# Two layers behind a causal attention on one core: layer 2's first product reads its tokens and its weights from tiles declared early in SBUF

## The chip, the cores and the metric

The kernel runs on one core of a Trainium2 chip. Its time is the device time of one execution in microseconds (us). Of the kernel before there are three timed runs and one profiled execution.

## The reference

Three stages in float32, cut to what is computed:

```
x = causal attention(q, k, v) with decay f      # 4 batches x 8 heads x 576 x 64
x = x as [2304 tokens, 512]
h = x @ w_in                                     # layer 1: 512 -> 1024
solu = h * softmax(h);  ln = layernorm(solu) * g_ln
x = ln @ w_out                                   # 1024 -> 512
h = max(x @ moe2_w_in, 0)                        # layer 2: 512 -> 2048
out = (h * h) @ moe2_w_out                       # 2048 -> 512
```

## The kernel before

Every float32 product is made of three matmuls of rounded halves (high x low, low x high, high x high), so a tile of operands always comes as an h and an l. Layer 2 works on blocks of TB = 256 tokens with Strassen-like products of blocks, which is why its weights are prepared as seven sums per unit (w2u in DRAM, 128x512 each) and its down weights as sums in w2d, w2f and w2s.

**Order.** Nothing is issued as the program text stands. Each piece of work is added to a `Plan` with costs, a due time (`prio`), the keys that it reads and writes, and the ring slots that it takes. `pl.lay` then simulates the five engines and writes one order for each; DMAs all go through SyncE's queue (SP). A changed key, ring size or cost can therefore move instructions on all engines.

**Layer 2** is made of four kinds of work:
- `half_up(p)` (matmul at L1300), eight of them: the first block's up product. Moving operands are XOP[5] and XOP[6] (tiles vn0 to vn3); weights are pieces of `HU`: first six pieces of `upper`, then wil, k20, k21, pt, e.
- `unit(b, p)`, 32 of them: seven products of six 128x256 matmuls each (`mm`, L1347). The stationary operand is a piece of the ring `upper`, loaded from w2u by the DMA at L1336; the moving operand is XOP[i], the token operand i of the block of tokens. Products 0 and 1 are opened together (`open2`: one matmul of product 1, the six of product 0, the other five of product 1). VectorE adds results out of PSUM (L1373), ScalarE and GpSimd make relu and square; a result takes a slot of the ring RQ.
- `step(blk, p)`, 72 of them: VectorE forms sums of a result (L1418) and its halves (L1111, `k<-adj,k` for the S half, `ln<-q,ln` for the A half), then TensorE does seven down products of three 128x256 matmuls (L1448, L1449, L1450). Stationary: GA (in ln1) or GS (in k11). Moving: halves of the down weights, in pieces of wih, free, woh, wil, k20, k21, pt, e, ws, q3, qn, xc and one last small piece of k11.
- `x_block(b)`: loads and splits the token operands of a block of 512 tokens into XOP (L1191 and behind).

**Where things lie.** Layer 2 has no tiles of its own. `carve` cuts pieces out of tiles of the earlier stages, and `once`/`claim` make the first user of a piece wait until the earlier stage's keys on it (`held`) are done. All tiles come from one pool with one buffer each, and lie in SBUF in the order of their declaration; in bytes of a partition:

| tiles, in order | bytes | role in layer 2 |
|---|---|---|
| maskb; wih, wil, woh | 1152; 2496 to 51648 | W2 pieces (moving) |
| wol; k20, k21, qn | 51648 to 92608 | XOP[1] to XOP[4]; W2 pieces |
| vn0 to vn5, kn0, kn1 | 92608 to 108992 | XOP[5], XOP[6]; raw loads |
| pt, e | 108992 to 125888 | W2 pieces, half_up weights |
| q2 | 125888 to 134080 | four RQ slots |
| free, ws, xc, q3 | 134080 to 158144 | W2 pieces |
| adj, xh, xl, ident, xw, x, q1 | 158144 to 182144 | sums, seven RQ slots, raw loads |
| k10, k11 | 182144 to 204672 | `upper`, GS |
| ln0, ln1 | 204672 to 229248 | `upper`; GA, one `upper` piece, XOP[0] |

In names of the trace the digits at a tile's end are cut: `k` is any of k10, k11, k20, k21, and `ln` is ln0 or ln1. Before the change `upper` has 13 pieces: five of k10, GS[4] of k11, six of ln0, GA[4] of ln1. Product i of unit n uses piece (7n + i) mod 13. XOP[0] is GA[5:7], the last 4096 bytes of ln1.

```
K1 = [new(f"k1{j}", [HH, KW], F32R) for j in range(2)]
GA = carve("ln1", [384] * 4 + [512] * 3)
XOP[0] = GA[5:7]
m = (7 * n + i) % NU
```

Of the kernel before, what the change touches and what calls it, by code (L numbers as in the profile page):

```python
# [240 lines left out]
def tile_kernel(ctx: ExitStack, tc: tile.TileContext, q, k, v, f, w_in, w_out, g_ln, w2_in, w2_out, out):  # L241
# [76 lines left out]
    X = new("x", [NP, P])  # L318
    Q1 = [[new(f"q1{i}{j}", [HH, P], F32R) for j in range(2)] for i in range(2)]
    K1 = [new(f"k1{j}", [HH, KW], F32R) for j in range(2)]  # L320
    for y in range(2):
        new(f"ln{y}", [KF * 3 * P])
    LN = {}
    XC = {}
    Z = [ps.tile([P, 512], F32, name=f"z{i}") for i in range(2)]
# [1 line left out]
    HP = ps.tile([P, 2, 512], F32, name="hp")  # L327
    PP = [ps.tile([P, 512], F32, name=f"pp{i}") for i in range(3)]

    NU, NRQ = 13, 11  # L330
    pl = Plan(dict(pp=3, hp=2, rq=NRQ), ("z0", "z1", "xo", "h", "h0", "h1"))
    uid = [0]

# [393 lines left out]
    def weights1(prio_in, prio_out):  # L727
        ws = {}
        n = 0

        for c in range(2):
            for r in range(KC):
                i = n % 4
                w = slice(c * 512, (c + 1) * 512)

                def stage(i=i):
                    tag = f"ln{i // 2}"
                    if tag not in ws:
                        ws[tag] = new(tag, [KF * 3 * P])
                    return ws[tag][:, (i % 2) * 1536 : (i % 2) * 1536 + 1536]  # L740

                convert(
                    w_in[r * P : (r + 1) * P, w].bitcast(U32), lambda stage=stage: stage()[:, 0:1024],
                    lambda stage=stage: stage()[:, 1024:1536], lambda r=r, w=w: wih[:, r, w],
                    lambda r=r, w=w: wil[:, r, w], 512, prio_in + n * PIN, ("lnr", i), ("lnw", i), ("wi", r, c),
                )
                n += 1
        for g in range(2 * KF):
            j, c = divmod(g, 2)
            i = g % 2  # L750
            w = slice(c * 256, (c + 1) * 256)

            def stage(i=i):
                tag = ("xc", "ws")[i]
                if tag not in ws:
                    ws[tag] = new(tag, [768])
                return ws[tag]

            convert(
                w_out[j * P : (j + 1) * P, w].bitcast(U32), lambda stage=stage: stage()[:, 0:512],  # L760
                lambda stage=stage: stage()[:, 512:768], lambda j=j, w=w: woh[:, j, w],
                lambda j=j, w=w: wol[:, j, w], 256, prio_out + g * POUT, ("wsr", i), ("wsw", i), ("wo", j, c),
                gain=gcol[:, j : j + 1],
            )
        return ws


    def out1(blk, ccs, prio, dp):
# [3 lines left out]
        for cc in ccs:  # L772
            w = slice(cc * P, cc * P + P)
            sk = key()
            for g in range(4):
                def fn(g=g, sk=sk, w=w):
                    px = at(sk)[:, 0 : 2 * P].rearrange("p (r x) -> p r x", x=P)
                    for fc in (2 * g, 2 * g + 1):
                        hi = LN["h"][:, fc, ring[0] : ring[1] + 1 : step, :]
                        lo = LN["l"][:, fc, ring[0] : ring[1] + 1 : step, :]  # L780
                        nc.tensor.matmul(px, lhsT=woh[:, fc, w], rhs=lo, start=(fc == 0), stop=False)  # L781
                        nc.tensor.matmul(px, lhsT=wol[:, fc, w], rhs=hi, start=False, stop=False)  # L782
                        nc.tensor.matmul(px, lhsT=woh[:, fc, w], rhs=hi, start=False, stop=(fc == KF - 1))  # L783
# [31 lines left out]
    def first(x):  # L815
# [82 lines left out]
        for g in range(KF // 4):  # L898
            ck = key()

            def flips(g=g, ck=ck):
                if not LN:
                    LN["h"], LN["l"] = (new(f"ln{y}", [KF, 3, P], F32R) for y in range(2))
                tp = at(ck).rearrange("p (c x) -> p c x", x=P)
                for c in range(4):
                    cc = 4 * g + c
# [1 line left out]

            def lo(g=g, ck=ck):
                nc.vector.tensor_tensor(  # L910
                    out=LN["l"][:, 4 * g : 4 * g + 4, x % 3, :], in0=at(ck).rearrange("p (c x) -> p c x", x=P),
                    in1=LN["h"][:, 4 * g : 4 * g + 4, x % 3, :].bitcast(F32), op=ALU.subtract,
                )

# [29 lines left out]
    for nm, a in (("h", "woh"), ("l", "wol")):  # L944
        held[a] = [("wo", fc, y, nm) for fc in range(KF) for y in range(2)]
    held["ln0"] = [("lnh", y, z) for y in range(3) for z in range(2)]
    held["ln1"] = [("lnl", y, z) for y in range(3) for z in range(2)]
    held["e"], held["x"] = ["e"], ["x"]
    held["xh0"], held["xl0"] = [("xh", 0, o) for o in (0, 64)], [("xl", 0, o) for o in (0, 64)]
    held["ws"] = [("wsr", 1, z) for z in "lh"] + [("wsw", 1)]  # L950
# [42 lines left out]
    upper += carve("k10", [512] * 5)  # L993
    GS = carve("k11", [512] * 5 + [256])
    upper += GS[4:5] + carve("ln0", [512] * 6)
    GA = carve("ln1", [384] * 4 + [512] * 3)
    upper += GA[4:5]
    XOP[0] = GA[5:7]
    at_h = len(large)
    more("wil", 8)  # L1000
    for j in range(2):
# [5 lines left out]
    more("qn", 0, 2)  # L1007
    more("xc", 0, 3)
    small += GS[5:]
    RQ = [carve(a, [512], F32)[0] for a in ["xl0", "xh0", "adj2"] + [f"q1{i}{j}" for i in range(2) for j in range(2)]]  # L1010
    RQ += carve("q2", [512] * 4, F32)
    U2 = [carve(a, [256], F32)[0] for a in ("xw", "maskb")]
    KP = KF2 // 2
    HU = upper[:6] + large[at_h:]
# [266 lines left out]

    def new_r(sg, p, prio):
        for x, y in enumerate(RQ):
            once(("rq", x), y, ["rqs"], prio)
        uid[0] += 1
        rslot[sg, p] = ("rq", uid[0])
        return rslot[sg, p]
# [25 lines left out]
    def unit(b, p, prio):  # L1313
# [12 lines left out]
        def half(i):  # L1326
            o = uprods[i]
            return psum(ks[o[0]])[:, o[1] * TB : o[1] * TB + TB]

        def weights(i, prio):  # L1330
            m = (7 * n + i) % NU
            sk = ("us", m)
            if sk not in first_use:
                once(sk, again(upper[m]), [sk], prio)
            pl.add(
                dict(dma=LOAD2), lambda: nc.sync.dma_start(upper[m][0]().bitcast(F32), w2u[p, i]), prio - UAHEAD,  # L1336
                [("w2u", p, i)], [sk],
            )
            return [sk, ("xo", i, 0), ("xo", i, 1)]

        def mm(i, a=0, e=6, start=-1):
            u, xh, xl = upper[(7 * n + i) % NU][0](), XOP[i][0][0](), XOP[i][1][0]()
            for j in range(a, e):
                c, k = divmod(j, 3)
                wh, wl = u[:, c * P : c * P + P], u[:, 256 + c * P : 256 + c * P + P]
# [272 lines left out]
            first(tiles[n]["x"])  # L1618


    t0 = TEND + P2
    t1 = t0 + KP * 2800
    x_half(t0 - W2X)
# [110 lines left out]
```

## Time and profile before

| | |
|---|---|
| three runs | 836.78, 838.57, 839.84 us; median 838.57 |
| profiled execution | 837.13 us, span 835.3 us |
| mean granted TensorE clock | 0.994 of full speed |
| TensorE (PE) busy | 791.1 us, 95% of the span, 6392 matmuls |
| weight loads (PEld) busy | 720.6 us, 86% |
| VectorE (DVE) busy | 635.1 us, 76% |
| ScalarE (ACT) busy | 549.3 us, 66% |
| GpSimd (POOL) busy | 394.3 us, 47% |
| chain that ended last | PE 69%, ACT 11%, DVE 8%, DMA 4% |

Attention and layer 1 run interleaved up to 488 us, with the eight half_up products between 453 and 488; from there on only layer 2 is left. A matmul's duration in a row includes the pipeline, so consecutive matmuls overlap; the pace is read from the distance of their starts.

### The profile page before, as it was taken

How to read it: one execution, taken by the hardware profiler on the slowest of the kernel's cores; microseconds unless marked ns; L12 is line 12 of the kernel's file. 1: busy time of each engine (PE TensorE's matmuls, PEld its weight loads, DVE VectorE, ACT ScalarE, POOL GpSimd, SP SyncE). 2: the span in 40 equal slices, each digit the busy share in tenths (PEclk: the TensorE clock that was granted, in tenths of full speed). 3: DMA queues.
4: the chain of work that ended last, by engine and by line, in shares of the span. 5: the costliest groups of instructions: out<-in, count | busy, mean ns of one | idle time of the engine just before them, and what ended most of it. 6: DMA issues, size and time to landing. Idle time of an engine off the chain costs nothing.

```text
span 835.3 us, 18703 instructions
## 1 busy us (share of the span) xinstructions
PE 791.1 (95%) x6392; PEld 720.6 (86%) x6392; DVE 635.1 (76%) x1614; ACT 549.3 (66%) x1414; POOL 394.3 (47%) x544
## 2 busy tenths in 40 slices
PE   4877899999999999999999998999999999999997
PEld 2555688888888788888889998999999999999997
DVE  8798867977867567776757789778778877977776
ACT  6899988888888888998866665444334433533342
POOL 6468777666688766798677310020211121112110
PEclk9999999999999999999999999999999999999999
DMA  6644346556655454655557789976766757665401
GB/s 204 207 135 127 110 122 202 176 170 203 182 177 191 153 185 133 208 201 189 198 181 230 250 284 345 319 259 212 218 191 232 234 180 230 203 209 180 162 8 44
DMA packets 109663, 159.66 MB, mean 191 GB/s; under 512 B 12832, under 2 KB 52768, under 8 KB 109568
## 3 DMA queue, kind: packets, MB, share of 16 engines
q1 hardware_dynamic: 109568, 158.47, 59.3%
q8 instruction: 50, 0.82, 0.4%
q14 instruction: 45, 0.37, 0.2%
HBM read 121.65 MB, written 36.72 MB: 190 GB/s over the span
## 4 chain that ended last, share of the span: by engine, by line
PE 69%; ACT 11%; DVE 8%; DMA 4%; POOL 3%; issue 3%; SPq 0%; DVEq 0%; POOLq 0%; ACTq 0%
PE z L1347 9%; PE pp L1347 9%; PE pp L592 5%; PE xo L612 5%; PE z L538 4%; PE hp L1449 3%; PE hp L1448 3%; PE hp L1450 3%; PE hp L830 3%; PE hp L832 3%; PE hp L831 3%; ACT adj L573 2%; PE pp L781 2%; PE pp L783 2%; PE pp L782 2%
## 5 line engine op out<-in xcount | busy, mean ns | idle before, releaser
L573 ACT ACTIVATE adj<-z,st 64x288 f32<-64x288 f32 (+9 forms) x192 | 95.3, 500 | 13.1 <-DVE st L559 9.7
L538 PE MATMUL z<-k,q 80*64 80x288 f32 (+17 forms) x384 | 93.9, 345 | 9.0 <-DVE q L503 8.3
L592 PE MATMUL pp<-ident,adj 128*128 128x128 f32 (+1 forms) x480 | 82.0, 282 | 17.0 <-ACT adj L573 15.7
L592 PEld LDWEIGHTS pp<-ident,adj 128*128 128x128 f32 (+1 forms) x480 | 52.1, 144 | 44.4 <-ACT adj L573 27.7
L559 DVE CUSTOM_DVE_ANT_0 z<-z,maskb 128x128 f32<-128x128 f32 (+8 forms) x144 | 65.5, 464 | 29.5 <-PE z L538 27.6
L781 PE MATMUL pp<-ln,woh 128*128 128x256 f32 x288 | 83.9, 291 | 1.5 <-DVE ln L910 1.5
L347 ACT COPY pt<-pp 128x256 f32<-128x256 f32 (+5 forms) x170 | 69.0, 419 | 18.8 <-PE pp L592 17.6
L1111 DVE TENSOR_TENSOR k<-adj,k 128x512 fp32r<-128x512 f32 x75 | 52.6, 701 | 37.7 <-POOL k L351 28.2
L783 PE MATMUL pp<-ln,woh 128*128 128x256 f32 x288 | 80.7, 280 | 0.0
L782 PE MATMUL pp<-ln,wol 128*128 128x256 f32 x288 | 80.7, 280 | 0.0
L538 PEld LDWEIGHTS z<-k,q 128*128 128x128 f32 (+3 forms) x384 | 58.1, 188 | 15.9 <-ACT pt L1554 8.2
L351 POOL TENSOR_SCALAR ln<-q 128x384 fp32r<-128x384 f32 x31 | 16.9, 545 | 107.0 <-PE hp L1450 45.8
L705 POOL TENSOR_TENSOR free<-free 128x256 uint32<-128x256 uint32 x64 | 50.5, 796 | 35.4 <-DVE free L699 28.6
L830 PE MATMUL hp<-wih,xl 128*128 128x512 f32 x144 | 62.1, 431 | 2.8 <-ACT hp L869 2.8
L612 PE MATMUL xo<-pt,vn 128*64 128x128 f32 (+1 forms) x960 | 63.8, 274 | 0.5 <-ACT pt L347 0.3
L612 PEld LDWEIGHTS xo<-pt,vn 128*64 128x64 f32 x960 | 50.6, 140 | 11.5 <-issue 6.1
L351 POOL TENSOR_SCALAR k<-adj 128x512 fp32r<-128x512 f32 x38 | 23.7, 622 | 75.1 <-DVE adj L1418 30.3
L781 PEld LDWEIGHTS pp<-ln,woh 128*128 128x128 f32 x288 | 54.8, 190 | 4.4 <-DVE ln L910 1.8
L831 PE MATMUL hp<-wil,xh 128*128 128x512 f32 x144 | 56.9, 395 | 0.2 <-DVE wil L709 0.2
L832 PE MATMUL hp<-wih,xh 128*128 128x512 f32 x144 | 56.9, 395 | 0.0
L782 PEld LDWEIGHTS pp<-ln,wol 128*128 128x128 f32 x288 | 55.0, 191 | 0.4
L783 PEld LDWEIGHTS pp<-ln,woh 128*128 128x128 f32 x288 | 54.8, 190 | 0.0
(580 smaller groups left out, 2636.3 us busy)
## 6 DMA issues: line engine op xcount, KB each, us to landing
ln<-w2u SPq DMA_DIRECT2D x119, 256.0 KB
k<-w2u SPq DMA_DIRECT2D x105, 256.0 KB
w2u<-free SPq DMA_DIRECT2D x56, 256.0 KB
kn<-in_k_dram SPq DMA_DIRECT2D x32, 256.0 KB
free<-in_moe_w_out_dram SPq DMA_DIRECT2D x32, 256.0 KB
free<-in_moe_w_in_dram SPq DMA_DIRECT2D x32, 256.0 KB
w2f<-free SPq DMA_DIRECT2D x49, 128.0 KB
vn<-in_v_dram SPq DMA_DIRECT2D x20, 256.0 KB
```

Of the source, the lines that this page charges most:

```text
L347: nc.scalar.copy(dst(), src())
L538: nc.tensor.matmul(dst, lhsT=ql[0:r, p, 0:m], rhs=rhs, start=(g == 0), stop=(g == 1))
L573: nc.scalar.activation(out=adj[0:m, c[1] : c[2]], in_=Z[c[0]][0:m, 0 : c[2] - c[1]], func=AF.Exp, bias=st[0:m, low : low + 1], scale=-1.0, ...
L592: nc.tensor.transpose(at(sk)[:, (c - g) * m : (c - g + 1) * m], adj[0:m, zc : zc + P], ident[0:m, 0:m])
L612: nc.tensor.matmul(XO[own[j], g // 2, off : off + m], lhsT=VN[vslot[b, c]][:, (g + j) * D : (g + j + 1) * D], rhs=PT[(s - h + g + j) % NPT ...
L781: nc.tensor.matmul(px, lhsT=woh[:, fc, w], rhs=lo, start=(fc == 0), stop=False)
L782: nc.tensor.matmul(px, lhsT=wol[:, fc, w], rhs=hi, start=False, stop=False)
L783: nc.tensor.matmul(px, lhsT=woh[:, fc, w], rhs=hi, start=False, stop=(fc == KF - 1))
L830: nc.tensor.matmul(HP[:, c], lhsT=XL[i][:, cc, :], rhs=wih[:, cc, w], start=(cc == 0), stop=False)
L831: nc.tensor.matmul(HP[:, c], lhsT=XH[i][:, cc, :], rhs=wil[:, cc, w], start=False, stop=False)
L832: nc.tensor.matmul(HP[:, c], lhsT=XH[i][:, cc, :], rhs=wih[:, cc, w], start=False, stop=(cc == KC - 1))
L1347: nc.tensor.matmul(half(i), lhsT=l, rhs=r[:, c * TB : c * TB + TB], start=(j == start), stop=(j == 5), skip_group_check=True,)
```

## The change

Three homes are moved. XOP[0], the moving operand of product 0, goes from ln1 to the second half of q2. The weights of product 0 leave the ring: unit n loads them into one of two pieces in the first half of q2 (`lower[n % 2]`). The ring `upper` keeps products 1 to 6 with 12 pieces (the piece in ln1 is dropped); product i uses piece (6n + i - 1) mod 12. In exchange RQ loses its four slots in q2 and gets three in ln1, ten in all in place of eleven; these three come first in the list and are held by empty steps until layer 1 ends. For that, ln1 is split in two tiles, ln1a (GA) and ln1b (RQ), at the same addresses, and layer 1's low half LN["l"] is a list of the two.

```diff
-    for y in range(2):
-        new(f"ln{y}", [KF * 3 * P])
+    new("ln0", [KF * 3 * P])
+    for y in "ab":
+        new(f"ln1{y}", [KF // 2 * 3 * P])
...
-    NU, NRQ = 13, 11
+    NU, NRQ = 12, 10
...
-                        lo = LN["l"][:, fc, ring[0] : ring[1] + 1 : step, :]
+                        lo = LN["l"][fc // 4][:, fc % 4, ring[0] : ring[1] + 1 : step, :]
...
-    held["ln1"] = [("lnl", y, z) for y in range(3) for z in range(2)]
+    for z in range(2):
+        held["ln1" + "ab"[z]] = [("lnl", y, z) for y in range(3)]
...
     GS = carve("k11", [512] * 5 + [256])
     upper += GS[4:5] + carve("ln0", [512] * 6)
-    GA = carve("ln1", [384] * 4 + [512] * 3)
-    upper += GA[4:5]
-    XOP[0] = GA[5:7]
+    GA = carve("ln1a", [384] * 4)
+    c = carve("q2", [512] * 4)
+    lower, XOP[0] = c[:2], c[2:]
...
-    RQ = [carve(a, [512], F32)[0] for a in ["xl0", "xh0", "adj2"] + [f"q1{i}{j}" for i in range(2) for j in range(2)]]
-    RQ += carve("q2", [512] * 4, F32)
+    RQ = carve("ln1b", [512] * 3, F32)
+    LATE = len(RQ)
+    RQ += [carve(a, [512], F32)[0] for a in ["xl0", "xh0", "adj2"] + [f"q1{i}{j}" for i in range(2) for j in range(2)]]
...
         for x, y in enumerate(RQ):
-            once(("rq", x), y, ["rqs"], prio)
+            if x >= LATE:
+                once(("rq", x), y, ["rqs"], prio)
...
+        def place_of(i):
+            if i == 0:
+                return ("ul", n % 2), lower[n % 2]
+            m = (6 * n + i - 1) % NU
+            return ("us", m), upper[m]
+
         def weights(i, prio):
-            m = (7 * n + i) % NU
-            sk = ("us", m)
+            sk, piece = place_of(i)
             if sk not in first_use:
-                once(sk, again(upper[m]), [sk], prio)
+                once(sk, again(piece), [sk], prio)
             pl.add(
-                dict(dma=LOAD2), lambda: nc.sync.dma_start(upper[m][0]().bitcast(F32), w2u[p, i]), prio - UAHEAD,
+                dict(dma=LOAD2), lambda: nc.sync.dma_start(piece[0]().bitcast(F32), w2u[p, i]), prio - UAHEAD,
                 [("w2u", p, i)], [sk],
             )
...
-            u, xh, xl = upper[(7 * n + i) % NU][0](), XOP[i][0][0](), XOP[i][1][0]()
+            u, xh, xl = place_of(i)[1][0](), XOP[i][0][0](), XOP[i][1][0]()
...
+    late = [("rq", f"late{x}") for x in range(LATE)]
+    for k_ in late:
+        pl.add(dict(dve=0), lambda: None, -9.1e6, [], [], take=k_)
+    pl.add(dict(dve=0), lambda: None, TEND, [], list(RQ[0][1]), uses=late)
```

Line numbers shift with it: L1336 becomes L1347, L1347 becomes L1358, L1448 to L1450 become L1459 to L1461, L1111 becomes L1116, L1373 becomes L1384, L1418 becomes L1429.

**TensorE, the opening of the first unit.** First as it stands before (the name ahead of the arrow is the PSUM bank, behind it the moving and the stationary tile):

```order
2326 L1347 MATMUL z_120<-wol_5725,k_49_5115 128x256
2327 L1347 MATMUL z_120<-ln_49_5597,k_49_5115 128x256 x6
2328 L1347 MATMUL z_120<-wol_5725,k_49_5115 128x256 x5
2329 L1347 MATMUL z_121<-wol_5725,k_49_5115 128x256 x12
2330 L1347 MATMUL z_120<-wol_5725,k_49_5115 128x256 x6
2331 L1347 MATMUL pp_126<-wol_5725,ln_49_5773 128x256
2332 L1347 MATMUL pp_126<-ln_49_5597,ln_49_5773 128x256 x6
2333 L1347 MATMUL pp_126<-wol_5725,ln_49_5773 128x256 x5
```

And now:

```order
2326 L1358 MATMUL z_121<-wol_5731,k_50_5121 128x256
2327 L1358 MATMUL z_121<-q_50_5025 128x256 x6
2328 L1358 MATMUL z_121<-wol_5731,k_50_5121 128x256 x5
2329 L1358 MATMUL z_122<-wol_5731,k_50_5121 128x256 x12
2330 L1358 MATMUL z_121<-wol_5731,k_50_5121 128x256 x6
2331 L1358 MATMUL pp_127<-wol_5731,ln_50_5779 128x256
2332 L1358 MATMUL pp_127<-q_50_5025 128x256 x6
2333 L1358 MATMUL pp_127<-wol_5731,ln_50_5779 128x256 x5
```

The six matmuls of product 0 stand at the same place, between the first and the other five of product 1. Before they read ln (XOP[0]) against weights in k (unit 0) or ln (unit 1); now both operands are in q2, which the row names once. Over the program TensorE has the same matmuls; their order differs within the first four units only, and from there to the end it is the same.

**SyncE's queue, the loads of product 0's weights for units 0 and 1.** Before, around the first loads of layer 2's down weights:

```order
302 L1131 DMA adj_49_5009<-w2d 128x512
303 L1179 DMA k_49_5022<-w2s 128x256
304 L1059 DMA w2u<-free_576 128x512 x4
305 L1131 DMA vn_49_5089<-w2d 128x512
306 L677 DMA free_576<-in_moe_w_in_dram 128x2x256 x2
```

And now:

```order
303 L1136 DMA adj_50_5012<-w2d 128x512
304 L1347 DMA q_50_5025<-w2u 128x512 x2
305 L1184 DMA k_50_5047<-w2s 128x256
306 L1064 DMA w2u<-free_578 128x512 x4
307 L1136 DMA vn_50_5095<-w2d 128x512
```

The two loads into q2 now stand between the load of w2d and that of w2s. Before, unit 0's stood as `k<-w2u` 28 rows further down (row 330) and unit 1's in the group `ln<-w2u x3` (row 357).

**VectorE around the operand halves of the first step of a unit's block** (L1111 and L1116 make halves, L1373 and L1384 add unit results out of PSUM). Before:

```order
894 L1111 TENSOR_TENSOR wil_5257<-adj_49_5009,wil_5257 128x512
895 L1111 TENSOR_TENSOR wil_5257<-kn_49_4457,wil_5257 128x512
896 L1111 TENSOR_TENSOR wil_5257<-kn_49_4472,wil_5257 128x512
897 L1373 TENSOR_TENSOR q_49_5805<-maskb_5900,pp_125 128x256
898 L1373 TENSOR_TENSOR q_49_5805<-q_49_5805,pp_125 128x256
899 L1111 TENSOR_TENSOR k_49_5022<-adj_49_5379,k_49_5022 128x512
900 L1111 TENSOR_TENSOR qn_5948<-vn_49_5089,qn_5948 128x256
901 L1111 TENSOR_TENSOR k_49_5240<-vn_49_5132,k_49_5240 128x512
```

And now:

```order
894 L1116 TENSOR_TENSOR wil_5263<-kn_50_4460,wil_5263 128x512
895 L1116 TENSOR_TENSOR wil_5263<-kn_50_4475,wil_5263 128x512
896 L1384 TENSOR_TENSOR maskb_5915<-maskb_5915,pp_127 128x256
897 L1116 TENSOR_TENSOR k_50_5047<-adj_50_5385,k_50_5047 128x512
898 L1384 TENSOR_TENSOR xl_50_5360<-maskb_5915,pp_126 128x256
899 L1384 TENSOR_TENSOR xl_50_5360<-xl_50_5360,pp_126 128x256
900 L1116 TENSOR_TENSOR qn_5952<-vn_50_5095,qn_5952 128x256
901 L1116 TENSOR_TENSOR k_50_5246<-vn_50_5138,k_50_5246 128x512
```

`k<-adj,k`, the S half of the first step, moved ahead of the two adds that read the bank pp (`q<-maskb,pp` and `q<-q,pp` before, `xl<-maskb,pp` and `xl<-xl,pp` now).

## Rows read from the trace of the kernel before

**Rows 1.** Windows of layer 2: us, busy us of each engine, clock, DMA share, GB/s.

```profile
488.00:500.00 12.00, 12.00 (x106) 12.00 (x105) 11.18 (x21) 9.50 (x20) 0.88 (x1) 1.00 0.93 304
500.00:520.00 20.00, 17.30 (x138) 16.40 (x138) 18.96 (x46) 12.09 (x24) 2.31 (x3) 1.00 1.01 336
520.00:536.00 16.00, 15.74 (x134) 15.53 (x133) 13.38 (x37) 7.35 (x16) 1.24 (x2) 1.00 0.94 326
536.00:816.00 280.00, 279.93 (x2373) 279.73 (x2371) 217.00 (x568) 110.95 (x225) 46.80 (x80) 1.00 0.61 197
816.00:836.00 20.00, 14.04 (x117) 13.84 (x117) 12.99 (x35) 3.99 (x7) 1.54 (x3) 0.97 0.08 27
```

**Rows 2.** Waits of TensorE, 420 to 836 us: us in total, times, longest.

```profile
PE xo L1448 <- DVE k L1111: 2.1, 2, 1.6
PE pp L1448 <- DVE k L1111: 0.7, 1, 0.7
PE pp L1347 <- DMA ln<-w2u: 0.6, 1, 0.6
...
PE z L1347 <- DVE q L1373: 0.3, 1, 0.3
```

**Rows 3.** Timeline of TensorE, 487 to 498 us: start, us, line, bank, moving, stationary.

```profile
487.61 0.88 PE L1300 MATMUL z<-vn,e 128*128 128x256 f32 x6
488.33 0.28 PE L1448 MATMUL hp<-free,ln 128*128 128x256 f32 x1
...
493.09 0.28 PE L1347 MATMUL z<-wol,k 128*128 128x256 f32 x1
493.20 0.88 PE L1347 MATMUL z<-ln,k 128*128 128x256 f32 x6
493.92 2.87 PE L1347 MATMUL z<-wol,k 128*128 128x256 f32 x23
496.63 0.28 PE L1347 MATMUL pp<-wol,ln 128*128 128x256 f32 x1
```

**Rows 4.** Timeline of TensorE, 504 to 506 us, idle time and releaser in brackets.

```profile
504.56 0.38 PE L1448 MATMUL xo<-woh,k 128*128 128x256 f32 x1 [1.57 <-DVE k L1111]
...
505.02 0.28 PE L1448 MATMUL pp<-free,k 128*128 128x256 f32 x1
...
505.96 0.28 PE L1450 MATMUL xo<-free,k 128*128 128x256 f32 x1
```

**Rows 5.** L1448 on TensorE, before 493 us and from 540: ns min/median/max.

```profile
L1448 PE MATMUL hp<-wih,ln x3: 276/276/276, 488.7 to 491.4; 128*128 128x256 f32 x3
...
L1448 PE MATMUL hp<-wih,ln x21: 279/279/279, 540.4 to 784.7; 128*128 128x256 f32 x21
```

**Rows 6.** Timeline of TensorE, the half_up products from 456 us.

```profile
456.60 0.88 PE L1300 MATMUL z<-vn,wil 128*128 128x256 f32 x6
457.32 0.84 PE L1300 MATMUL z<-vn,k 128*128 128x256 f32 x6
458.00 0.88 PE L1300 MATMUL z<-vn,wil 128*128 128x256 f32 x6
```

**Rows 7.** L1449 on TensorE, 540 to 816 us: ns min/median/max.

```profile
L1449 PE MATMUL hp<-k,ln x35: 280/280/290, 544.7 to 807.4; 128*128 128x256 f32 x35
```

**Rows 8.** Timeline of SyncE's queue at 427, 459 and 487 us.

```profile
427.43 0.40 SPq L1179 DMA_DIRECT2D k<-w2s  x1
430.85 2.40 SPq L1059 DMA_DIRECT2D w2u<-free  x4
...
458.99 0.42 SPq L1336 DMA_DIRECT2D k<-w2u  x1
...
487.14 1.33 SPq L1336 DMA_DIRECT2D ln<-w2u  x3
```

**Rows 9.** L538 on TensorE, the readers of q2, 420 to 440 us.

```profile
L538 PE MATMUL z<-k,q x8: 292/296/382, 421.8 to 425.8; 128*128 128x288 f32 x4, 80*128 80x288 f32 x4
```

**Rows 10.** Timeline of VectorE, an add of a unit.

```profile
503.03 0.42 DVE L1373 TENSOR_TENSOR q<-maskb,pp 128x256 f32<-128x256 f32 x1 [0.42 <-PE pp L1347]
```

More of the change, by code (lines that the diff above doesn't have):

```diff
@@ L736, in stage @@
                 def stage(i=i):
-                    tag = f"ln{i // 2}"
+                    tag = ("ln0", "ln0", "ln1a", "ln1b")[i]
                     if tag not in ws:
-                        ws[tag] = new(tag, [KF * 3 * P])
-                    return ws[tag][:, (i % 2) * 1536 : (i % 2) * 1536 + 1536]
+                        ws[tag] = new(tag, [KF // (1 + i // 2) * 3 * P])
+                    o = i % 2 * 1536 if i < 2 else 0
+                    return ws[tag][:, o : o + 1536]
                 convert(
@@ L902, in flips @@
                 if not LN:
-                    LN["h"], LN["l"] = (new(f"ln{y}", [KF, 3, P], F32R) for y in range(2))
+                    LN["h"] = new("ln0", [KF, 3, P], F32R)
+                    LN["l"] = [new(f"ln1{y}", [KF // 2, 3, P], F32R) for y in "ab"]
                 tp = at(ck).rearrange("p (c x) -> p c x", x=P)
@@ L910, in lo @@
                 nc.vector.tensor_tensor(
-                    out=LN["l"][:, 4 * g : 4 * g + 4, x % 3, :], in0=at(ck).rearrange("p (c x) -> p c x", x=P),
+                    out=LN["l"][g][:, :, x % 3, :], in0=at(ck).rearrange("p (c x) -> p c x", x=P),
                     in1=LN["h"][:, 4 * g : 4 * g + 4, x % 3, :].bitcast(F32), op=ALU.subtract,
```

## The prediction

> **What bounds the kernel now.** I read the page's busy table, then stretches of layer 2, then the waits of TensorE there, then single matmul starts. Layer 2's units and down steps run from 488 us to the end, and in [rows 1] its middle is one engine: from 536 to 816 us TensorE is busy 279.93 of 280 us with 2373 matmuls, at a granted clock of 1.00 (the 2.4 GHz level); VectorE has 217.00 us, ScalarE 110.95, the DMA engines a share of 0.61. [Rows 2] lists all that TensorE waited for from 420 us on: 2.1 and 0.7 us for VectorE's operand halves, 0.6 us for a DMA of unit weights, 0.3 us for a unit's bank; only that last one falls into the middle. So a buffer that comes free earlier buys nothing there. What can move this stage is the pace of back-to-back matmuls, and the opening from 488 to 520 us, where VectorE is busy 18.96 of 20 us.
>
> **The pace is not one number.** All these matmuls are 128x256, with a new stationary tile each, at clock 1.00. Take starts that follow without a wait and divide by the count.
> - Just before the units, the down products of block 0 run 42 matmuls from 488.33 to 493.09 us: 4.76/42 = 113.3 ns [rows 3].
> - From 493.92 to 496.63 us, 23 unit products: 2.71/23 = 117.8 ns [rows 3]. Eight down products from 505.02 to 505.96 us: 117.5 ns [rows 4]. The middle as a whole: (280 - 0.3)/2373 = 117.9 ns [rows 1, 2].
> - The six of a product 0 from 493.20 to 493.92 us: 120 ns [rows 3]. The six with e from 487.61 to 488.33 us: also 120 ns [rows 3].
>
> What differs is where the two operands lie. Call the tiles declared from k10 on high, and those up to q3 low. Down products and products 1 to 6 have their moving operand low and the stationary one high: mixed sides. Product 0 moves XOP[0] out of ln1 against weights in k10, k11, ln0 or ln1: both high. The half_up products on wil, pt and e move vn tiles: both low. One side costs 120 ns. Mixed sides have two lasting paces, 113.3 and 117.7, and the durations of the down products show which one holds: 276 ns for every L1448 matmul before 493 us, 279 for every one after 540 [rows 5].
>
> What chooses the pace is what ran just before. After both low, the mixed ones run at 113.3 at once: wil x6 at 456.60, k x6 at 457.32, wil at 458.00, so six mixed ones took 0.68 us, 113.3 ns [rows 6]; and e x6 at 487.61 is followed by the 42 at 113.3 [rows 3]. After both high they run at 117.8: 493.20 is the first product 0, 493.92 the first stretch at that pace [rows 3], and with a product 0 every 10 us the longer durations go on to the end [rows 5]. The pace of 117.7 then outlasts a pause: the restart at 504.56 us, after 1.57 us of waiting, leads into 117.5 [rows 4].
>
> **The change, part by part.**
> 1. *Product 0 becomes both low.* Its token operands go to q2's second half, its weights to q2's first. In TensorE's order the same six matmuls stand at the same place. q2 lies between e and free, and e moves nothing here but free does at 488.33 at 113.3 [rows 3], so I take q2 as low. Own pace of product 0: 120 before and 120 after, by the six on e [rows 3]; bounds 119.5 to 121, some 0.2 us either way over 32 of them.
> 2. *The pace after it.* Each product 0 should now leave the pace of 113.3, as wil and e do. Of the 32 units 27 open behind 536 us (four at 493, 497, 512, 524 us and one just ahead of it stand before), so 162 of the 2373 matmuls are products 0 and 2211 remain. Their pace is (279.7 - 162 x 0.120)/2211 = 117.7 ns; at 113.3 they gain 4.4 ns each: 2211 x 4.4 = **9.7 us**. From 524 to 536 us, where TensorE hardly waits either [rows 1], 11 us at 117.8 ns are 93 more: 0.4 us. VectorE has room: 217 us of work in then 270.
> 3. *What may take the 113.3 away.* A product 0 comes every 10 us, so whatever spoils the pace does so for 10 us at most. Once a block one down product keeps both operands high (the last piece of k11 as W2); it is the long end of the row 280/280/290 [rows 7]. It comes about 2.5 us ahead of the next product 0 but for the last block: 6 x 2.5/0.118 x 4.4 ns = 0.56 us, plus 0.3 us after 807. Between 0 and 0.9 us of loss I take **0.5**. The single wait of the middle is one more restart, inside the same bound.
> 4. *Opening, 488 to 520.* The first two product-0 weights were loaded at 458.99 us and in the three ln loads at 487.14; now both are issued at 427, where SP issues nothing from 427.83 to 430.85 us [rows 8] and q2 has been read for the last time at 425.8 [rows 9]. Two issues of 0.4 us fit in that gap, and TensorE's list of waits has none near it [rows 2], so I cost them at nothing; if they blocked SP, the next issues would be the w2u stores at 430.85. The saturated stretch loses 256 KB, some 0.8 us at its 336 GB/s [rows 1]. That attacks the DMA wait of 0.6 us; but next comes the 1.57 us wait for VectorE's operand half [rows 4], and VectorE is nearly full. The change also puts that half (k<-adj,k) ahead of two adds of the unit of 0.42 us each [rows 10], so it is due some 0.8 us sooner, but that order pushes the adds back by as much. Bounds 0 and -2.2 us (both waits gone); VectorE's load decides, so I take **-0.4**.
> 5. *Rings.* Weights: 13 pieces for seven products become 12 for six plus 2 homes. Results: 11 slots become 10. TensorE's order behind the first four units is unchanged, and TensorE's middle shows no wait for a ring [rows 2], so nothing; a ring that is late would show as TensorE waiting for a w2u DMA, or for VectorE behind a slot. Price bound: 0 to 2 us.
> 6. *Tail, 816 to the end.* TensorE is busy 14.04 of 20 us, behind VectorE [rows 1], and no product 0 is left: 0. The split of ln1, and the empty steps that hold three late slots, issue nothing: 0.
>
> Sum on the profiled run: 837.13 - 9.7 - 0.4 + 0.5 - 0.4 = 827.1 us. That run is 1.44 us under the median 838.57, so the forecast on the median is **828.6 us**.
>
> **Where a rule speaks against this.** In the rows the same matmul at the same clock takes 113.3, 117.7 or 120 ns by where its operands lie [rows 3]. The Trainium skill, page "TensorE: Matmul & The Clock Gate", section "Step-by-step: what each phase is for", says that the two operands come through independent read ports and that loading the next weights takes no read bandwidth from the running matmul; "SBUF — State Buffer", section "Who interferes with whom", has "PE and ACT never wait on anyone." By that the home of an operand is indifferent and only the opening counts. The 120 against 113.3 in [rows 3] does not agree with it.
>
> **The rivals.**
> - *The pace stays at 117.7.* Another cause than product 0 sets it. For it: a restart at 117.5 after a pause [rows 4], and the stretch at 113.3 ends as DMA and VectorE fill up, shares 0.93 and 1.01 [rows 1]. Against: the middle has a DMA share of 0.61 and is still at 117.7, and 457.32 and 488.33 turn to 113.3 at once. Then only part 4 is left: 838.57 - 0.4 = 838.2; 836.5 to 839.5. The rule above gives this too.
> - *The pace holds part of the time.* Copies of new token operands or writes into q2, or some restart, throw it back until the next product 0; half of term 2, or a ring wait of part 5 on top: 838.57 - 4.9 - 0.4 = 833.3; 832 to 836.
> - *Slower: both low leaves 120 behind.* The place is the same exit of product 0. If, after six both-low matmuls, the mixed ones stuck at the one-side pace, 2211 x 2.3 ns = 5.1 us come on top: 843.7 us. It decides as soon as the exit pace is above 117.7 in more than half of the products. For it: I have only two such exits at this place in rows, and one lasts just six matmuls. Against: both are 113.3, to the last of 42 [rows 3, 6].
>
> **How the numbers follow.** Forecast 0.62 (826 to 831.5), part of the time 0.10, pace unchanged 0.20, slower 0.08. About 0.3% (2.5 us, so 836.1 and 841.1) is what a measurement here can tell from no change. Faster: 0.62 + 0.09 = 0.71; same: 0.20 + 0.01 = 0.21; slower 0.08. Low end: 837.13 - 9.9 - 0.4 - 2.2 on the profile, 826.1 on the median, and half a microsecond for the spread of runs (836.78 to 839.84): 825.5. High end: 838.2, which takes in the second case and half of the third and leaves about 2 in 10 out.
>
> **What the profile after would show.** Right: L1459 at 276 ns throughout the units, six product-0 matmuls at 283 and 120 ns apart, the next start 113 ns after; the 2373 matmuls of the middle in about 270 us; no new wait. Wrong: 279 with starts 118 apart (first rival), runs of 279 that begin at an identifiable event (second), 283 everywhere (third), or a TensorE wait for w2u or for VectorE in the middle (part 5).

## The result and the profile after

The changed kernel takes **827.38 us** (median of 6 runs, 825.16 to 831.46) against 838.68 us (6 runs, 836.78 to 839.84) for the kernel before: ratio 0.9869, 95% interval 0.9841 to 0.9897. The forecast was 828.6 us in a range of 825.5 to 838.2. The profiled execution took 827.87 us, span 826.1, mean granted clock 0.992; before it was 837.13 us. Of the 9.3 us between the two profiles 0.9 lie ahead of layer 2 (its first down product starts at 487.39 us, before at 488.33), the rest in it.

The windows of layer 2 after, with columns as in [rows 1]; the middle now ends 10 us sooner, so it is cut at 806:

```profile
488.00:500.00 12.00, 11.74 (x102) 11.54 (x101) 10.82 (x20) 9.19 (x20) 1.19 (x1) 1.00 0.83 268
500.00:520.00 20.00, 17.29 (x138) 16.23 (x137) 18.73 (x47) 11.62 (x24) 2.75 (x4) 1.00 1.02 340
520.00:536.00 16.00, 16.00 (x140) 16.00 (x139) 11.39 (x32) 7.34 (x16) 1.24 (x2) 1.00 0.99 359
536.00:806.00 270.00, 269.91 (x2360) 269.70 (x2359) 215.08 (x569) 110.42 (x227) 46.75 (x80) 1.00 0.63 201
806.00:826.00 20.00, 14.66 (x123) 14.26 (x121) 13.73 (x38) 4.31 (x8) 1.54 (x3) 0.94 0.09 31
```

TensorE is as full as before (269.91 of 270 us), at the same clock, with almost the same number of matmuls: 2360 in 270 us are 114.4 ns each, where 2373 in 280 us were 118.0. So nothing was hidden or shortened; the matmuls follow each other faster. The list of TensorE's waits from 420 us on answers to [rows 2]:

```profile
PE xo L1459 <- DVE k L1116: 2.1, 2, 1.3
PE pp L1459 <- DVE k L1116: 0.7, 1, 0.7
PE pp L1358 <- ACT k L348: 0.4, 1, 0.4
PE z L1358 <- DVE xw L1384: 0.3, 1, 0.3
```

The DMA wait of 0.6 us is gone; VectorE's operand halves are waited for as long as before, and 0.4 us for ScalarE are new. TensorE's timeline at the first units, against [rows 3]:

```profile
487.39 0.28 PE L1459 MATMUL hp<-free,ln1a 128*128 128x256 f32 x1
...
492.15 0.28 PE L1358 MATMUL z<-wol,k 128*128 128x256 f32 x1
492.26 0.88 PE L1358 MATMUL z<-q 128*128 128x256 f32 x6
492.98 2.09 PE L1358 MATMUL z<-wol,k 128*128 128x256 f32 x17
495.33 0.97 PE L1358 MATMUL z<-wol,k 128*128 128x256 f32 x6 [0.26 <-DVE xw L1384]
```

Product 0 (z<-q) has its 120 ns as before: 492.26 to 492.98 is 0.72 us for six. Behind it 17 matmuls fill 2.09 us; less the 0.276 us of the last one, the 16 distances are 113.4 ns. Before, the same place ran at 117.8. The down products show the same in their durations, 276 ns where [rows 5] had 279, and product 0 keeps 283:

```profile
L1459 PE MATMUL hp<-wih,ln1a x21: 276/276/276, 539.1 to 775.8; 128*128 128x256 f32 x21
...
L1358 PE MATMUL pp<-q x84: 280/283/287, 536.1 to 786.4; 128*128 128x256 f32 x84
```

Not all of layer 2 is at 113.3. Once a block, at its eighth step, a stretch at 117.8 begins:

```profile
527.15 0.28 PE L1459 MATMUL hp<-xc,ln1a 128*128 128x256 f32 x1
527.27 0.28 PE L1460 MATMUL hp<-k,ln1a 128*128 128x256 f32 x1
527.39 0.28 PE L1461 MATMUL hp<-xc,ln1a 128*128 128x256 f32 x1
...
529.75 0.89 PE L1358 MATMUL z<-q 128*128 128x256 f32 x6
530.47 2.87 PE L1358 MATMUL z<-wol,k 128*128 128x256 f32 x23
533.18 0.28 PE L1459 MATMUL xo<-e,k 128*128 128x256 f32 x1
...
536.12 0.88 PE L1358 MATMUL pp<-q 128*128 128x256 f32 x6
536.84 0.39 PE L1358 MATMUL pp<-wol,ln 128*128 128x256 f32 x2
```

The matmul at 527.27 is the both-high one of [rows 7]. The product 0 at 529.75 does not end the stretch: the 23 behind it need 533.18 - 530.47 = 2.71 us, 117.8 ns each. Only the one at 536.12 does. Of the 32 groups of product 0 in the whole trace, 16 found the pace of 113.3 and all of these kept it; 16 found 117.8, and 7 of these brought 113.3 back. So a product 0 in q2 keeps 113.3 where it finds it, and brings it back from 117.8 only sometimes.

### The profile page after: what moved, and what is told of

Its sections match the earlier page's. It is cut to its first block, busy times and chain, and to the rows that moved or that the text cites. A ratio compares the mean times of both kernels' runs of the same rounds, so it can differ in the third digit from the quotient of the medians.

```text
span 826.1 us, 18710 instructions
## 1 busy us (share of the span) xinstructions
PE 783.4 (95%) x6392; PEld 712.8 (86%) x6392; DVE 631.2 (76%) x1612; ACT 548.3 (66%) x1415; POOL 394.6 (48%) x545
## 4 chain that ended last, share of the span: by engine, by line
PE 70%; ACT 10%; DVE 8%; DMA 5%; POOL 3%; issue 3%; SPq 0%; DVEq 0%; POOLq 0%; ACTq 0%
PE z L1358 9%; PE pp L1358 9%; PE pp L593 6%; PE xo L613 5%; PE z L539 5%; PE hp L832 3%; PE hp L834 3%; PE hp L833 3%; PE hp L1461 3%; PE hp L1460 3%; PE hp L1459 3%; PE pp L783 3%; PE pp L784 2%; PE pp L785 2%; ACT adj L574 2%
## 5 line engine op out<-in xcount | busy, mean ns | idle before, releaser
L785 PE MATMUL pp<-ln,woh 128*128 128x256 f32 x288 | 80.5, 280 | 0.0
L1116 DVE TENSOR_TENSOR k<-adj,k 128x512 fp32r<-128x512 f32 x75 | 53.0, 706 | 36.0 <-POOL k L352 26.9
L785 PEld LDWEIGHTS pp<-ln,woh 128*128 128x128 f32 x288 | 54.6, 190 | 0.0
L1358 PE MATMUL z<-wol,k 128*128 128x256 f32 x384 | 52.6, 277 | 0.3 <-DVE xw L1384 0.3
L1069 POOL TENSOR_TENSOR free<-free 128x256 f32<-128x256 f32 x64 | 50.4, 788 | 4.2 <-DMA w2d<-free 0.9
L1358 PE MATMUL pp<-wol,ln 128*128 128x256 f32 x384 | 52.0, 278 | 0.4 <-ACT k L348 0.4
```

The lines of the kernel that those rows point to most:

```text
L1358: nc.tensor.matmul(half(i), lhsT=l, rhs=r[:, c * TB : c * TB + TB], start=(j == start), stop=(j == 5), skip_group_check=True,)
```

## The experiments

The theory on record was of sides: operands that both lie high cost 120 ns and leave 117.8 behind, both low leave 113.3. Twelve kernels tested it; it missed on the first and fell on the fifth.

**1. The last piece of the down weights goes low.**

```
-    small += GS[5:]
+    small += carve("maskb", [256])
-    U2 = [carve(a, [256], F32)[0] for a in ("xw", "maskb")]
+    U2 = [carve(a, [256], F32)[0] for a in ("xw", "adj2")]
```

> The changed kernel, but the last small piece of the down weights (moving operand of one down product per block, high against high) lies in maskb, low; the unit's second scratch takes adj2 in its place, and the ring of results has 9 slots. Theory: that one both-high matmul per block is what throws the 113.3 ns pace back to 117.8. Then the 20 to 61 mixed matmuls behind it stay at 113.3, down products last 276 ns throughout from 550 us on, and some 313 matmuls x 4.4 ns = 1.4 us come off the units' middle: 825 to 827 us. Rival (the pace is lost at the start of a block's steps whatever the operand's home): 117.8 behind the same place as before, 827 to 829 us.

Measured: 830.99 us, ratio 0.9904 (0.987 to 0.9938), above both ranges; in its profile layer 2 begins only at 490.87 us, and from there it lasts 339.0 us against 338.7 in the changed kernel. The trace has the rival's outcome: the stretch at 117.8 begins at the very same matmul, although its moving operand now lies at byte 1152, the lowest of all. The timeline at one block's eighth step:

```profile
614.18 0.28 PE L1459 MATMUL hp<-xc,ln1a 128*128 128x256 f32 x1
614.29 0.28 PE L1460 MATMUL hp<-maskb,ln1a 128*128 128x256 f32 x1
614.41 0.28 PE L1461 MATMUL hp<-xc,ln1a 128*128 128x256 f32 x1
614.53 0.28 PE L1459 MATMUL hp<-e,ln1a 128*128 128x256 f32 x1
```

The starts are 0.11 us apart up to 614.29, then 0.12. Either the place in the block does it, or "high" was the wrong name for what maskb and k11 share.

**2 to 4. Product 0's tokens and weights on other sides.** In all three RQ, the ring of results, gives up or gets slots (9, 9 and 11) to make room.

```
# 2: tokens high, weights low
+    d = carve("ln1b", [512] * 3)
+    lower, XOP[0] = carve("q20", [512] * 2), d[:2]
# 3: weights high, tokens low
+    d = carve("ln1b", [512] * 3)
+    lower, XOP[0] = d[:2], carve("q20", [512] * 2)
# 4: both high, two homes, a ring of 11 without product 0
+    d = carve("ln1b", [512] * 3)
+    lower, XOP[0] = [d[2], GS[4]], d[:2]
```

> The changed kernel with product 0's tokens in the high tile ln1b and its weights low in q2 (9 slots of results): product 0 then has mixed sides the other way round. Theory (both high sets 117.8, both low preserves or restores 113.3): product 0 itself runs below 120, the pace is 113.3 until the first both-high down product at about 527 us, and with no both-low product left nothing restores it: middle at 117 to 118 ns, 834 to 838 us. Rival (only both-high inside product 0 matters): 113.3 nearly throughout, 825 to 828 us. Rival (a high moving operand is what slows): 117.8 from the first product 0 on, 837 to 839 us.

> The changed kernel with product 0's weights in the high tile ln1b and its tokens low in q2 (9 slots of results): product 0 becomes like products 1 to 6. Theory: product 0 runs at the pace of its neighbours; after the first both-high down product (about 527 us) or a restart at the longer pace nothing restores 113.3, so 117.8 from there on: 834 to 837 us. Rival (the both-high product 0 of the kernel before was the only cause): 113.3 throughout with product 0 at 113.3 too, 825 to 827 us.

> The changed kernel's structure (two homes for product 0's weights, a ring without product 0, 11 pieces) but all four homes high: tokens and one home in ln1b, the other home in k11; q2 keeps four slots of results. Theory: product 0 is both high again, every mixed matmul behind it at 117.8 and down products at 279 ns, 835 to 839 us. Rival (the gain is from the homes, the loads or the order, not from the side): 826 to 829 us.

Measured: 837.29 us (ratio 0.9981, 0.9961 to 1.0), 839.59 us (0.9999, 0.9977 to 1.0021) and 839.14 us (1.0007, 0.9986 to 1.0027). The fourth keeps the two homes of product 0's weights and a ring without it, and with product 0 high again the old time is back. It does not keep the early loads (its first load for product 0 is at 483.31 us, in the changed kernel at 426.67) nor the order of the first units, which is that of before; the seventh below has this same order and late loads and is faster all the same, and the ninth has the changed kernel's order and early loads and is not. TensorE's order from the seventh unit on is one and the same in the kernel before, the fourth and the changed kernel. From the first matmul of the seventh unit to the last of the 32nd there are 2162 matmuls; by their starts they take 255.15 us before, 255.15 in the fourth, 247.21 in the changed kernel. The third shows what a product 0 like its neighbours is worth: after a restart at 500.35 us the pace is 117.8 and nothing brings 113.3 back, 2162 matmuls in 254.65 us; its time lies above the range expected. The second lies in the range of the theory, but not for its reason: it did something that no theory on record had. Product 0 with the homes exchanged turns the pace over, from 532 us on each time:

```profile
599.91 0.86 PE L1359 MATMUL pp<-ln1b,q 128*128 128x256 f32 x6
600.61 2.09 PE L1359 MATMUL pp<-wol,ln 128*128 128x256 f32 x17
```

These 17 belong to a stretch of 78 at 113.4 ns, which follows 138 at 117.8; the next product 0 turns it back to 117.8, and so on to the end.

**5. A map of homes.** TensorE alone, one large tile, operands at chosen addresses:

```
+    for st in (24 * K, 116 * K, 188 * K, 215 * K):
+        for m in MS:
+            for _ in range(12):
+                mm(m, st)
```

> None of the reference is computed: TensorE alone runs 128x256 matmuls without a wait, first 12 in a row for each of 29 homes of the moving operand (1,152 to 225,000 bytes of a partition) against four homes of the stationary one (24, 116, 188 and 215 KB); then, 29 times, 12 with both low, 12 mixed, one with the moving operand at the home under test against a stationary one at 215 KB, 12 mixed. Theory: the pairs fall in two classes, 120 ns where both lie on one side and 113 to 118 where they don't, with one border between 158 and 166 KB; a single both-high matmul turns the 12 behind it to 117.8 and a single mixed one doesn't. Rival (the first experiment's reading): a home at the very start of SBUF behaves like a high one, so the map has more than one border and 1,152 stands at 120 against 188 and 215 KB.

Measured: neither. Whatever the home, the starts are 120.0 ns apart, from 8 KB to 220 KB against all four stationary homes (118.8 to 121.2 for the three below 4 KB). One row for 1003 of them:

```profile
L51 PE MATMUL z<-big x1003: 279/283/290, 59.8 to 180.0; 128*128 128x256 f32 x168
```

So sides mean nothing for the pace of a stretch. What these addresses have in common is that all but one (2500) are multiples of 128 bytes. From 4 KB on they are multiples of 256 too; 1152 and 2176 are not, and the twelve matmuls there ran at 119.0 and 118.8 ns against each stationary home. In the kernel the "low" tiles of the table of addresses (wih at 2496, wol, vn, pt, e, q2, free, xc) all start at 64 modulo 128, the "high" ones (k10, k11, ln0, ln1) at 0, and maskb at 1152, the odd one out of the first experiment, at 0 too. Modulo 256 they are as sharply divided: 192 for all the low ones, 128 for the high ones and maskb. So a rule of 128 bytes and one of 256 can't be told apart there either.

**6. The both-high matmul at another step.**

```
     small += GS[5:]
+    small[7], small[15] = small[15], small[7]
```

> The changed kernel with two small pieces of down weights exchanged: the last one (in k11, high) serves the fourth step of each block, and the fourth step's piece in ws (low) serves the eighth. If the both-high matmul itself throws the pace to 117.8, the 117.8 stretch begins at the fourth step of every block and the eighth stays at 113.3; if something about the eighth step of a block does it (its place, its stop flags, its loads), the stretches begin where they did, at the eighth step. Time within 1 us of the changed kernel's 827.4 either way.

Measured (a single run): 831.49 us, above what was expected. The 117.8 stretch moved with the piece, from the eighth step to the fourth of every block (554.82, 593.50, 632.18 us and so on), and the eighth stays at 113.3. So it is this matmul and not its place. Its stretches are longer there (20, then 78 matmuls behind a product 0), 2162 matmuls take 249.05 us.

**7 to 9. The theory of 64 bytes.** Three kernels move pieces by 64 bytes; the orders on all engines are those of the fourth (7) and of the changed kernel (8 and 9). Unused words of q3 make room. The padding moves other operands as well: in 7, ln1b comes ahead of ln0, and k10 and the first four pieces of k11 lie 128 bytes lower; in 8, k10 and k11 lie 128 bytes lower; in 9, free, ws, xc and q3 lie 128 bytes higher.

```
# 7: both high, but at 64 modulo 128
+    new("ln1b", [KF // 2 * 3 * P + 16])
+    GS = carve("k11", [512] * 4 + [16, 512, 256])
# 8: last piece of the down weights at 64 modulo 128
+    GS = carve("k11", [512] * 5 + [16, 256])
# 9: both in q2, but at 0 modulo 128
+    c = carve("q2", [16] + [512] * 4)[1:]
```

> The both-high version again (its order on every engine is the same), but padded so that product 0's tokens, both homes of its weights and the last small piece of the down weights start 64 bytes off: their addresses are 64 modulo 128 like those of wol, vn and q2, while the ring's k10 and ln0 stay at 0. New theory (the first experiment broke the one of sides): it is the address modulo 128 bytes, both operands in the same class cost 120 ns, both at 0 modulo 128 throws the pace to 117.8, both at 64 keeps 113.3. Then it behaves like the changed kernel or better, with 276 ns durations: 824 to 829 us. Theory of low and high sides: product 0 is both high, 279 ns, 836 to 840 us.

> The changed kernel, its order on every engine kept, with the last small piece of the down weights (in k11) moved 64 bytes up, so that no matmul of the down products has both operands at 0 modulo 128. New theory: the 117.8 stretches behind the eighth step of each block go, some 313 matmuls x 4.4 ns = 1.4 us of the middle: 825 to 827 us, durations 276 from about 540 us on. Theory of sides: this piece is still high against high, the stretches stay, 827 to 828 us.

> The changed kernel, its order on every engine kept, with product 0's four pieces in q2 moved 64 bytes up: still low, but at 0 modulo 128. New theory: each product 0 has both operands at 0 modulo 128 and throws the pace to 117.8, as before the change: 836 to 840 us, durations 279. Theory of sides: both low as in the changed kernel, 826 to 829 us.

Measured: 832.25 us (ratio 0.9905, 0.9879 to 0.9931), 829.64 us (0.9878, 0.9851 to 0.9905) and 836.3 us (0.9961, 0.9939 to 0.9982). The times of the seventh and ninth fall as the theory of 64 bytes has it and not as that of sides: the seventh, high and at 64 modulo 128, needs 247.72 us for the 2162 matmuls, about as the changed kernel; the ninth, low and at 0, needs 254.29, nearly as before the change. But the traces don't show that product 0 does it. In the seventh, what follows a product 0 goes by where the next weights lie, in ln0 or in k10:

```profile
608.73 0.87 PE L1361 MATMUL z<-ln1b 128*128 128x256 f32 x6
609.43 2.17 PE L1361 MATMUL z<-wol,ln 128*128 128x256 f32 x17
...
618.47 0.88 PE L1361 MATMUL pp<-ln1b,k 128*128 128x256 f32 x6
619.18 2.09 PE L1361 MATMUL pp<-wol,k 128*128 128x256 f32 x17
```

Less the last one's 0.28 us, the first 17 have 118.2 ns and the second 113.4. So it is throughout: of the 32 groups of product 0, 17 are followed by weights in ln0, and behind all 17 the pace is 117.8, though 16 of them had found 113.3; 15 are followed by weights in k10, the tile that lies 128 bytes lower, and 13 of them keep 113.3. "Both at 64 keeps 113.3" fails there, and it is only with weights in k10 or k11 that 113.3 comes back after three or more matmuls at 117.8 (22 of 22 times between 525 and 805 us). So the seventh's gain hangs on tiles that were moved by 128 bytes. In the ninth the pace is lost before any product 0 has run:

```profile
489.96 0.88 PE L1306 MATMUL z<-vn,e 128*128 128x256 f32 x6
490.68 0.28 PE L1459 MATMUL hp<-free,ln1a 128*128 128x256 f32 x1
...
495.63 0.28 PE L1358 MATMUL z<-wol,k 128*128 128x256 f32 x1
```

These 42 down products take 4.95 us, 117.8 ns each, where the kernel before [rows 3] and the changed one need 4.76; the first of them moves free, which lies 128 bytes higher here, and in every other profile with this layer it runs at 113.3. So neither run moves product 0 alone by 64 bytes, and both have the pace change with a shift of 128 bytes, which a rule modulo 128 does not allow.

The seventh missed its time, because its layer 2 began at 492.03 us; from there it lasts 339.5 us against 338.7 in the changed kernel. The eighth missed too: other stretches at 117.8 came, among them around matmuls on xc and e, and the 2162 matmuls take 247.62 us. It had also moved k10 and k11 by 128 bytes, hence the eleventh.

**10. A map of offsets.**

```
+            for _ in range(n1):
+                mm(60 * K + 64, 190 * K)
+            for _ in range(n2):
+                mm(60 * K + 64, 30 * K + 64)
```

> None of the reference is computed: TensorE alone runs 128x256 matmuls without a wait; 18 in a row for moving operands at 60 KB plus 0 to 320 bytes against stationary ones at 190 KB plus 0, 32, 64 or 96; then homes from 2 to 200 KB, each at 0 and at 64 bytes, against stationary ones at 24, 116 and 215 KB; then mixed stretches with one matmul of both at 0, six or twelve of both at 64, of the classes exchanged, and of both at 0 between them. New theory: the pitch depends on the difference modulo 128 alone, 120 ns where it is 0, 113 to 118 where it is 64, whatever the home; stretches behind both-at-0 run at 117.8, behind both-at-64 they keep the pace they had or go back to 113.3. Theory of sides: 64 bytes change nothing, 120 or 113 by the home.

Measured: for 15 pairs of homes the starts are 119 to 120 ns apart with both at 0 modulo 128, and 117.6 in each with the moving operand 64 further. Then stretches with classes 64 and 0: behind a single matmul with both at 0, behind six with both at 64, behind six with the classes exchanged, and behind six with both at 0. The rows show the first, the second and the last:

```profile
L51 PE MATMUL z<-big x29: 279/279/280, 212.0 to 215.3; 128*128 128x256 f32 x29
...
L51 PE MATMUL z<-big x29: 276/276/278, 216.6 to 219.8; 128*128 128x256 f32 x29
...
L51 PE MATMUL z<-big x19: 279/279/280, 225.3 to 227.5; 128*128 128x256 f32 x19
```

Six or twelve with both at 64 lead into 113.3 in all nine rounds; the exchanged classes lead back to 117.8 in all nine. The stretch ahead of the single matmul was at 117.8 already, so this run does not show that it throws the pace. But it has the cleanest test of sides against bytes: the six with both at 64 and the six with both at 0 lie in the same two homes, at 60 and 30 KB, both low, 64 bytes apart, and both find 117.8 ahead of them. The first lead into 113.3 nine times of nine, the second leave 117.8 in all eight rounds that go on behind them. Here 64 bytes decide, with the homes, the pace ahead and the matmuls behind the same.

The first part of the run has multiples of 64 as well. The moving operand at 64, 128, 192 and 256 bytes beyond 60 KB, against weights at 190 KB, 18 matmuls each:

```profile
L51 PE MATMUL z<-big x17: 278/279/280, 35.8 to 37.7; 128*128 128x256 f32 x17
...
L51 PE MATMUL z<-big x16: 274/280/287, 44.4 to 46.2; 128*128 128x256 f32 x16
L51 PE MATMUL z<-big x15: 276/276/279, 46.6 to 48.2; 128*128 128x256 f32 x15
L51 PE MATMUL z<-big x16: 274/283/283, 48.6 to 50.4; 128*128 128x256 f32 x16
```

From the fourth matmul of each on, the starts are 117.8, 118.1, 113.4 and 119.5 ns apart. By a rule of 128 bytes the second would be as the fourth, and the first as the third. Offsets that are no multiple of 64 gave 113 to 120 ns, and stretches of 18 were too short to read a rule from.

**11 and 12. The last piece alone, beside the changed kernel.**

```
-    new("q3", [640])
+    new("q3", [576])
+    K1.append(new("k11", [HH * KW + 64], F32R)[:, 0 : HH * KW].rearrange("p (h x) -> p h x", x=KW))
+    GS = carve("k11", [512] * 5 + [16, 256])
```

> The changed kernel, its order on every engine kept, with the last small piece of the down weights 64 bytes further as in the eighth experiment, but padded so that every other operand of layer 2 keeps its address modulo 256 bytes (there k10 and k11 had moved by 128). Theory: the matmul with both operands at 0 modulo 128 is what begins the 117.8 stretch at a block's eighth step; without it some 300 matmuls of the middle gain 4.4 ns, 1.3 us against the changed kernel run beside it: 825 to 827.5 us. If the stretches stay, the modulo of 128 is not the whole rule, and the time is the changed kernel's within 0.5 us.

> The changed kernel itself, unaltered, on the same chip and against the same runs of before as the version beside it: 826 to 829 us, its layer 2 338 to 340 us long, with 117.8 stretches of 38 to 61 matmuls behind each block's eighth step as in its first profile.

Measured: 830.28 us (ratio 0.9886, 0.9864 to 0.9908) and 829.59 us (0.9887, 0.9865 to 0.9909), both above the ranges expected. In the trace of the eleventh the stretches are gone; an eighth step again, now at one pace:

```profile
615.84 0.28 PE L1461 MATMUL hp<-xc,ln1a 128*128 128x256 f32 x1
615.95 0.28 PE L1462 MATMUL hp<-k,ln1a 128*128 128x256 f32 x1
616.07 0.28 PE L1463 MATMUL hp<-xc,ln1a 128*128 128x256 f32 x1
616.18 0.28 PE L1461 MATMUL hp<-e,ln1a 128*128 128x256 f32 x1
```

The 2162 matmuls take 246.07 us against 247.21, the same figure in both profiles of the changed kernel: 1.1 us where 1.3 was expected. That the one matmul with both operands at 0 modulo 128 begins the stretch is shown by this and the sixth run together; in the eleventh this piece moves by 64 bytes modulo 256, and no other operand of layer 2 does. The total does not show it: the eleventh's layer 2 started at 493.16 us in its profile, where from 100 to 200 us the granted clock was 0.93:

```profile
100.00:200.00 100.00, 96.32 (x772) 0.93 0.54 164
```

against 0.97 (x787) in the twelfth. A microsecond in layer 2 is below what the whole time resolves here, so no version is shown to beat the changed kernel.

## Why the prediction was right, and where it was not

- *The bound.* Right: the middle is TensorE's pace alone; its length fell by as much as the pace, and VectorE took it, 215 us of work in 270.
- *The pace after product 0* (part 2). The size was about right, the reason wrong. "Each product 0 should now leave the pace of 113.3, as wil and e do" held for 23 of the 32, but I took low and high for the cause. The fifth run gives 120.0 ns at every home from 8 to 220 KB, and the tenth shows six matmuls with both low that lead into 113.3 or not by 64 bytes. In the kernel before, sides and addresses modulo 128 (and 256) went together for every tile that TensorE reads in layer 2, so no row could tell them apart. That q2, picked for its side, starts where it works was luck. What the runs don't have is the changed kernel with product 0 alone moved by 64 bytes: the ninth, which gains only 0.9 of the 7.9 us over the 2162 matmuls, had lost the pace to another tile before. Also, product 0 keeps 113.3 but does not always bring it back (529.75 against 536.12).
- *What may take the 113.3 away* (part 3). The culprit was right, its size too small: I took 0.5 us with an end at 0.9, counting 2.5 us, some 21 matmuls, until the next product 0. The pace comes back only with the second one, 38 to 50 matmuls later in the middle. Between unit 7 and unit 32 there are 2162 - 156 = 2006 matmuls besides product 0, which would have gained 8.8 us at 4.4 ns; they gained 7.9, so this cost 0.9 there alone, and the eleventh run got 1.1 back.
- *Product 0's own pace* (part 1): 120 before and 119.8 after, as taken.
- *The opening* (part 4): taken as 0.4 us, and 0.4 more from 524 to 536 us. From the first down product to the seventh unit it took 58.7 us before (488.33 to 547.07) and 58.2 after (487.39 to 545.56): 0.6 us, where 0.8 was taken up to 536 us and the 4.4 ns of part 2 are some 0.4 more from there to 547. So it gave half of what was forecast: a restart at 495.33 us, after 0.26 us of waiting, led from 113.3 into 117.8, and the stretch from 527.27 to 536.12 was at 117.8 too. The DMA wait went, VectorE's stayed at 2.1 us, as argued.
- *Rings and tail* (parts 5 and 6): no wait for a weight load or a slot came; what lies behind the last unit is 0.2 us longer, by what is left of the 8.3 us.
- *The rivals.* "The pace stays" did not come, but its argument, a restart at 117.5 after a pause, was a good hint: a restart can set the pace without a product 0, and 117.8 lasts until something ends it. In the third run both happen: 113.3 up to the wait at 500.35 us, 117.8 behind it for 300 us. "Slower: both low leaves 120 behind" never happened. The Trainium skill's page "TensorE: Matmul & The Clock Gate", section "Step-by-step: what each phase is for", with its independent read ports, would make all homes alike. For homes the fifth run agrees (120.0 from 8 to 220 KB); for 64 bytes the tenth and the eleventh do not (113.3 against 117.8 ns).
- The forecast came out 1.2 us from the median, closer than its terms, and in part by luck: they sum to 10.0 us for layer 2, which gained 8.3 (347.0 to 338.7 us). Another 0.9 us came from ahead of it, where kernels of the same order start layer 2 anywhere between 487.4 and 493.2 us in their profiles.

## What to carry to other kernels

Where TensorE is full, divide starts by counts stretch by stretch: a second pace at the same clock is worth as much as a removed wait. Before believing in a home, move the piece by 64 bytes and leave it where it is, and look at what the padding moves along: here 128 bytes on other tiles spoiled two such tests, and only the starts in their traces told. For back-to-back float32 matmuls with a new 128x128 stationary tile each, operands in different halves of 128 bytes avoid the 120 ns, but that alone does not give 113.3: in the third run all but one matmul of a block lie so, and the pace is 117.8 for 300 us. What kept 113.3 here, and sometimes brought it back, were groups of six with both operands at 192 modulo 256, between matmuls that move from 192 against weights at 128. Look for such a group, and for the single matmuls that lose the pace.

## What the runs showed that I had not expected

- The pace of a 128x256 float32 matmul at clock 1.00 depends on where its operands start within 256 bytes: 119 to 120 ns in stretches where the addresses are equal modulo 256, 118 to 119 where they are 128 apart (fifth and tenth run), 113.3 or 117.8 where they are 64 or 192 apart. The home made no difference: 120.0 from 8 to 220 KB, 117.6 for 15 pairs of homes 64 bytes apart.
- 113.3 and 117.8 are lasting states of the same instructions. In the changed kernel one matmul with both at 0 modulo 128 throws 113.3 to 117.8 for 38 to 68 matmuls. Six with both at 192 modulo 256 keep 113.3 there (16 of 16) and bring it back in 7 of 16; in the tenth run six with both at 64 modulo 256 brought it back in nine of nine rounds, in the seventh they lost it in front of weights in ln0 (17 of 17). Exchanged classes turn one into the other (second run). A restart after a wait went either way: in the changed kernel into 117.8 at 495.33 us, into 113.3 at 517.83.
- Why there are two states, by what rule of addresses they follow one another, what decides whether a product 0 restores 113.3 in the kernel, and what the matmuls on xc and e met in the eighth run, where k10 and k11 stood 128 bytes elsewhere, stay open.
